# Reordering VectorE sums around the token products and the changes of batch in a routed-attention and MLP-mixer kernel

## The chip, the core and the metric

The kernel runs on one core of one Trainium2 chip. The metric is the device time of one launch in microseconds. Before the change it is 838.61 us, the median of three runs that lie between 838.55 and 838.67 us. The profiled execution took 838.92 us, of which the profile's span, from the first to the last instruction, is 837.0 us, at a granted TensorE clock of 0.999 of full speed.

## What is computed

Two blocks follow each other. The first is attention with a routing mask: 4 batches, 8 heads, 768 positions, 64 values per head; a query sees only the keys that have the same nearest centroid. The second is an MLP mixer over the 4 x 768 x 512 result. The change touches only the second:

```python
def _moe_ref(x, w_tok1, w_tok2, w_ch1, w_ch2):      # x: (4, 768, 512)
    xt = x.transpose(0, 2, 1)
    h = np.maximum(xt @ w_tok1, 0.0) @ w_tok2       # 768 -> 256 -> 768, along the tokens
    u = x + h.transpose(0, 2, 1)
    h2 = np.maximum(u @ w_ch1, 0.0) @ w_ch2         # 512 -> 1536 -> 512, along the channels
    return (u + h2).astype(np.float32)
```

All of it is float32 on the chip.

## The kernel before

The matrix products of the mixer are done by Winograd's form of Strassen's scheme: both factors are cut into 2 x 2 blocks, and seven block products replace eight. It needs sums of blocks of the left factor (S1 to S4) and of the right factor (T1 to T4) beforehand, and VectorE (DVE in the profile) makes them. T3 and S3 are written over a block that is not needed afterwards. Three of the seven products of the first channel matrix are themselves split once more in the same way; the kernel calls these the sets, with sums of their own in narrower tiles.

```python
def winograd_left(a):
    yield lambda: add(a["S1"], a["A21"], a["A22"])
    yield lambda: sub(a["S2"], a["S1"], a["A11"])
    yield lambda: sub(a["S3"], a["A11"], a["A21"])
    yield lambda: sub(a["S4"], a["A12"], a["S2"])

def winograd_right(b):
    yield lambda: sub(b["T1"], b["B12"], b["B11"])
    yield lambda: sub(b["T2"], b["B22"], b["T1"])
    yield lambda: sub(b["T3"], b["B22"], b["B12"])
    yield lambda: sub(b["T4"], b["B21"], b["T2"])
```

`left_sums(part)` makes S1 to S4 of one third of w_ch1 (four instructions of 128 x 512), `u_sums()` makes T1 to T4 of u transposed (four of 128 x 768), `set_right_sums()` the sums of u for the sets (four of 128 x 384, then four of 128 x 192), and `token_sums` those of the hidden layer of the tokens (four of 128 x 512). `winograd_left` and `winograd_right` are lists of steps, so that a step can be placed among other work: `between()` takes one step from the list `others` after each product.

The seven products accumulate in PSUM banks and are taken out step by step: a product whose bank already holds an earlier one may start only after VectorE has added that earlier state to its destination.

```python
def by_turns(n, product, of, done=None, last=False, after=()):
    # order: p1 0, p1 1, p1 2, p5 0, p5 1, p5 2, c11 0, c11 1, u2 0, u2 1, u2 2, c12 0, c12 1,
    #        c22 0, c22 1, c22 2, c12 2, c11 2, c21 0, c21 1, c21 2
    for m in range(len(order) // 2):
        ...
        if name in FIRST:                       # p1, p5, c11 begin a bank
            banks[tag, i] = ptile(tag, n)
        product(banks[tag, i], a, r, i, name in FIRST)
        x = of(to, i)
        add(x, banks[tag, i], x)                # VectorE, from PSUM
        ...
        if m in after:
            after[m]()
        between()
```

The token products run for two batches at a time, first b = 0 and 1, then 2 and 3. Beside those of 2 and 3 ScalarE (ACT) copies u of batch 0 for its transposition by DMA (`turning`), and the last pieces of w_ch2 are rounded to float32 (`weights`):

```python
for b in (0, 2):
    tok1(b, 0)                                  # 12 matmuls, then a relu on ACT
    ...
    tok1(b, 1)
    take(weights, 2)
    if b == 2:
        take(turning, 4)                        # copies of u, on ACT
    tok1(b + 1, 0)                              # the third relu
    token_sums(b, 0)                            # T1
    take(weights, len(weights) if b == 2 else 1)
    if b == 2:
        left_weights()
        take(list(left_sums(0)), 4)             # S1 to S4 of w_ch1, first third
        nc.sync.dma_start(spill, xs[1])         # x of batch 1 to DRAM, 1.5 MB
    tok1(b + 1, 1)                              # the fourth relu
    token_sums(b, 1)                            # T2, T3, T4
    if b == 2:
        take(turning, len(turning))
        usums = u_sums()
        tok2_chunks(b, {13: lambda: (next(usums), next(usums))})
    else:
        tok2_chunks(b)
        turning = list(u_steps(0))
```

After that the four batches go through the channel matrices, in the order 0, 2, 3, 1, each in three parts of w_ch1 and w_ch2. `ch1_pair` makes the first product of a part and `ch2_chunks` the second:

```python
for n, b in enumerate(batches):
    for part in range(3):
        ...
        if first:
            others += [lambda: next(usums)] * 2
            for steps in (right_weights(0), left_sums(1), set_left_sums(1)):
                others += steps
        ch1_pair(part, not first, ...)
        ...
        if part == 2 and not last:
            after[3] = lambda: take(turning, len(turning))
            after[15] = lambda: next(usums)     # T1 of the next batch's u
            usums = u_sums()
        ch2_chunks(b, part, last, after)
        between(len(others))
        if part == 2 and not last:              # the change of batch
            for _ in range(3):
                next(usums)                     # T2, T3, T4
            for step in set_right_sums():       # eight steps
                step()
```

The head of `ch1_pair` at a change of batch, in the order of its products:

```python
big(X[0], "A11", "B11", 0); big(X[1], "A11", "B11", 1)   # each big() calls between()
big(Z[0], "S1", "T1", 0)
set_(yc[:, n0], "Y", "c11"); set_(yc[:, n1], "Y", "c12")
add(a11[:, 0], yc, a11[:, 0])
set_x("Y", "Y", "p1", a11[:, 0, n0])            # product, then the add from its bank
big(Z[1], "S1", "T1", 1)
set_x("Y", None, "u2", a11[:, 0, n1])           # same bank: waits for the add above
set_z("Y", ptile("Y", HS // 2), a11)
big(X[0], "S2", "T2", 0)
...
set_x("Y", None, "c22", ...); ...               # needs T3 of the sets
big(X[1], "S2", "T2", 1)
set_x("Y", None, "c21", ...); ...               # needs T4 of the sets
```

Of the kernel before, what the change touches and what calls it, by code (L numbers as in the profile page):

```python
# [50 lines left out]
def kernel(  # L51
# [29 lines left out]
    nc = tc.nc  # L81
# [51 lines left out]
    spill = spilled.tile([P, NJ, DM], F32, name="spill")  # L133
    xs = [(x1pool if b == 1 else xpool).tile([P, NJ, DM], F32, name=f"x{b}") for b in range(B)]
# [415 lines left out]
    def sub(dst, a, b):  # L550
        nc.vector.tensor_tensor(out=dst, in0=a, in1=b, op=ALU.subtract)
# [4 lines left out]
    def left_weights():  # L556

        w = W["ch1"]
        half = DCH // 2
        A = pools["A"] = {  # L560
            f"A{i + 1}{j + 1}": w[:, 2 * j : 2 * j + 2, half * i : half * i + half]
            for i in range(2)
            for j in range(2)
        }
        extra = pools["wsums"].tile([P, 3, 2, half], F32, name="w1s")
        A["S1"], A["S2"], A["S4"] = (extra[:, i] for i in range(3))
        A["S3"] = A["A21"]
# [13 lines that stand above are left out]
    def left_sums(part):  # L581

        cols = slice(part * P, part * P + P)
        return winograd_left(
            {k: x.rearrange("p f (r c) -> p f r c", r=2)[:, :, :, cols] for k, x in pools["A"].items()}
        )
# [3 lines left out]
    def set_lefts():  # L590
        if "l2" not in pools:
            pools["l2"] = pools["w2sums"].tile([P, 3, 3, HS], F32, name="w1ss")
        A, l2 = pools["A"], pools["l2"]
        both = W["ch1"].rearrange("p f (i r c) -> p f i r c", i=2, r=2)[:, 2:4]
        single = A["S4"].rearrange("p f (r c) -> p f r c", r=2)
        for blocks, sums_ in (
            ([both[:, f, :, r] for r in range(2) for f in range(2)], [l2[:, 0:2, m] for m in range(3)]),
            ([single[:, f, r] for r in range(2) for f in range(2)], [l2[:, 2, m] for m in range(3)]),
        ):
            yield dict(  # L600
                zip(("A11", "A12", "A21", "A22", "S1", "S2", "S4", "S3"), blocks + sums_ + blocks[2:3])
            )

    def set_left_sums(part):
        cols = slice(part * P, part * P + P)
        for blocks in set_lefts():
            yield from winograd_left({k: x[..., cols] for k, x in blocks.items()})
# [13 lines left out]
    def set_right_sums():  # L621
        pools["r2"] = pools["w2sums"].tile([P, 3, 3, HS // 2], F32, name="uTss")
        for blocks in set_rights():
            yield from winograd_right(blocks)
# [33 lines left out]
    def right_weights(part):  # L658


        w = W["ch2"]
        if part == 0:
            extra = pools["w2sums"].tile([P, 3, NCT // 2, DM // 2], F32, name="w2s")
            B_ = pools["B"] = {
                f"B{i + 1}{j + 1}": w[:, 6 * i : 6 * i + 6, 256 * j : 256 * j + 256]
                for i in range(2)
                for j in range(2)
            }
            B_["T1"], B_["T2"], B_["T4"] = (extra[:, i] for i in range(3))
            B_["T3"] = B_["B12"]  # L670
        b = {name: x[:, part : NCT // 2 : NCT // 4] for name, x in pools["B"].items()}
        yield lambda: sub(b["T1"], b["B12"], b["B11"])
        yield lambda: sub(b["T2"], b["B22"], b["T1"])
        yield lambda: sub(b["T3"], b["B12"], b["B22"])
        yield lambda: sub(b["T4"], b["B21"], b["T2"])
# [23 lines left out]
    def u_steps(b):  # L699


        order = (0, 1, 4, 5, 6, 7, 2, 3)
        for i in order[:UCOLS]:
            yield lambda i=i: u_take(b, i)
        for m, i in enumerate(order):
            yield lambda i=i: u_put(i)
            if m + UCOLS < len(order):
                yield lambda m=m: u_take(b, order[m + UCOLS])
# [15 lines left out]
    late, others = [], []  # L724
# [32 lines left out]
    def tok2_chunks(b, after=()):  # L757

        A, R = pools["AT"], pools["RT"]

        def product(psum, a, r, i, start):
            nc.tensor.matmul(  # L762
                psum, lhsT=A[a][:, i], rhs=R[r], start=start, stop=True,
                skip_group_check=not start,
            )

        def of(to, i):
            return xs[b + int(to[2]) - 1][:, HJ * (int(to[1]) - 1) + i]

        by_turns(DM, product, of, after=after)  # L770
# [321 lines left out]
    def take(steps, n):  # L1092
        for _ in range(n):
            steps.pop(0)()


    for b in (0, 2):
        tok1(b, 0)
        if b == 0:
            take(weights, 1)  # L1100
            pair_put(NPAIR - 1)
            pair_out(NPAIR - 1)
            assert not state
            attention.close()
            pools["wsums"] = pool("wsums", 1, side="right")
            pools["u"] = pool("upool", 1, side="right")
            token_stack = fast.enter_context(ExitStack())
            pools["tsums"] = pool("tsums", 1, token_stack, side="right")
            take(list(token_weights()), 4)
        else:  # L1110
            take(turning, UCOLS)
            take(weights, 2)
        tok1(b, 1)
        take(weights, 2)
        if b == 2:
            take(turning, 4)
        tok1(b + 1, 0)
        token_sums(b, 0)
        take(weights, len(weights) if b == 2 else 1)
        if b == 2:  # L1120
            left_weights()
            take(list(left_sums(0)), 4)
            nc.sync.dma_start(spill, xs[1])
        tok1(b + 1, 1)
        token_sums(b, 1)
        if b == 2:
            take(turning, len(turning))
            usums = u_sums()
            tok2_chunks(b, {13: lambda: (next(usums), next(usums))})
        else:  # L1130
            tok2_chunks(b)
            turning = list(u_steps(0))
    assert not weights
    token_stack.close()
# [5 lines left out]
    for n, b in enumerate(batches):  # L1140
        turning = []
        for part in range(3):
            first, last = n == 0 and part == 0, n == B - 1 and part == 2
            if part == 2 and not last:
                turning = list(u_steps(batches[n + 1]))
            if first:
                others += [lambda: next(usums)] * 2
                for steps in (right_weights(0), left_sums(1), set_left_sums(1)):
                    others += steps
            ch1_pair(part, not first, [turning.pop(0) for _ in turning[:UCOLS]])  # L1150
            if first:
                others += list(set_right_sums()) + list(right_weights(1))
            if n == 0 and part == 1:
                for steps in (left_sums(2), set_left_sums(2), right_weights(2)):
                    others += steps
            if n == 0 and part == 2:
                others += set_left_sums(0)
            if last:
                both = fits_load()
            after = {}  # L1160
            if part == 2 and not last:
                after[3] = lambda: take(turning, len(turning))
                after[15] = lambda: next(usums)
# [3 lines that stand above are left out]
            if n == 0 and part < 2:  # L1167
                (fits_count if part else fits)()
            if part == 2 and not last:
                for _ in range(3):  # L1170
                    next(usums)
                for step in set_right_sums():
                    step()
                if n == 0:
                    xs[1] = xpool.tile([P, NJ, DM], F32, name="x0")
                    nc.sync.dma_start(xs[1], spill)
# [212 lines left out]
```

## Time and profile before

| what | value |
|---|---|
| time, median of 3 | 838.61 us |
| span of the profile | 837.0 us |
| TensorE (PE) matmuls busy | 820.4 us, 98% |
| VectorE busy | 606.3 us, 72% |
| ScalarE busy | 381.3 us, 46% |
| 315 to 356 us, token products of batches 0 and 1 | PE busy 41.00 of 41.00 us |
| 356 to 398 us, token products of batches 2 and 3 | PE busy 39.28 of 42.00 us |
| 398 to 472 us, channel products, first batch, parts 0 and 1 | PE busy 72.42 of 74.00 us |
| 472 to 837 us, the rest | PE busy 354.88 of 365.00 us |

In the lines of the timeline shown below, a line begins with the start and the length in us, then come the engine, the line of the kernel, the operation, the tile written and those read, partitions x elements, and the count of instructions merged into the line; brackets at the end give the idle time of the engine before it and who ended it. In the list of waits, a line gives the engine that waited, its line, the engine and line that ended the wait, the total in us, how often, and the longest. A matmul's listed end is modelled, so the distance from one start to the next is the better measure of its cost: it is 0.43 us for a 128 x 512 matmul of the token products, for instance (six start in 2.58 us).

### The profile page before, as it was taken

The page shows a single profiled execution, that of the slowest core. Times are in us where ns is not written, and L with a number is a line of the kernel's source. Part 1 is how long each engine was busy: PE and PEld are TensorE (multiplying, and loading weights), DVE is VectorE, ACT ScalarE, POOL GpSimd, SP SyncE. Part 2 cuts the span into 40 slices and gives each one's busy share as a digit, 9 for nine tenths or more (in the row PEclk, how much of TensorE's full clock was granted, in tenths as well). Part 3 has the DMA queues.
Part 4 walks back from the last instruction along what each step waited for, and adds up shares of the span by engine and source line. Part 5 has one row for each costly group of instructions (what it writes and reads, how often), then busy time and mean ns, then how long its engine had stood idle before and what let it go on. Part 6 is the DMA issues. An engine that isn't in the chain of part 4 may idle for free.

```text
span 837.0 us, 11463 instructions
## 1 busy us (share of the span) xinstructions
PE 820.4 (98%) x4285; PEld 526.1 (63%) x4285; DVE 606.3 (72%) x1124; ACT 381.3 (46%) x562; POOL 30.7 (4%) x28
## 2 busy tenths in 40 slices
PE   9999999999999999998999999999999999999996
PEld 5444444444444444443578787878878788787875
DVE  6879898989898878749786676655667456664654
ACT  5678677787877774054202253121541204511120
POOL 1001010101101000000000000000000000000000
PEclk9999999999999999999999999999999999999999
DMA  9887566868675335034000125000230001400002
GB/s 152 150 149 152 119 139 129 166 131 161 145 141 127 83 95 150 20 79 123 0 1 1 19 39 170 1 0 10 38 105 1 1 1 28 123 1 0 1 2 79
DMA packets 184256, 63.39 MB, mean 76 GB/s; under 512 B 172800, under 2 KB 176896, under 8 KB 183936
## 3 DMA queue, kind: packets, MB, share of 16 engines
q1 hardware_dynamic: 182592, 62.18, 34.4%
q8 instruction: 35, 0.57, 0.3%
q10 hardware_dynamic: 1600, 0.39, 0.2%
q14 instruction: 29, 0.24, 0.1%
HBM read 36.21 MB, written 7.86 MB: 53 GB/s over the span
## 4 chain that ended last, share of the span: by engine, by line
PE 86%; DVE 7%; ACT 2%; DMA 2%; issue 1%; SPq 0%; ACTq 0%; DVEq 0%
PE sc L419 19%; PE av L444 14%; PE pX L940 13%; PE pX L788 11%; PE pZ L940 6%; PE pY L801 4%; PE pY L940 3%; PE ph L523 3%; PE pZ L788 3%; PE pZ L801 3%; DVE x L554 2%; PE pX L801 2%; DMA ucols<-urows 1%; PE small L480 1%; PE pX L762 1%
## 5 line engine op out<-in xcount | busy, mean ns | idle before, releaser
L426 ACT ACTIVATE ex<-sc 128x768 f32<-128x768 f32 x192 | 151.0, 812 | 28.9 <-PE sc L419 16.9
L419 PE MATMUL sc<-qkT 64*128 64x384 f32 x768 | 155.0, 482 | 0.0
L434 DVE TENSOR_TENSOR sum<-sum,ex 128x768 f32<-128x768 f32 x128 | 127.8, 998 | 26.9 <-ACT ex L426 14.3
L444 PE MATMUL av<-ex,va 128*64 128x384 f32 x768 | 127.4, 488 | 0.0
L554 DVE TENSOR_TENSOR x<-pX,x 128x256 f32<-128x256 f32 (+1 forms) x168 | 76.2, 459 | 41.2 <-PE pX L940 39.7
L444 PEld LDWEIGHTS av<-ex,va 128*64 128x64 f32 x768 | 53.7, 137 | 71.8 <-issue 65.9
L419 PEld LDWEIGHTS sc<-qkT 64*128 64x128 f32 x768 | 67.9, 187 | 38.4 <-issue 38.3
L828 ACT COPY hA<-pX 128x384 f32<-128x384 f32 x24 | 11.5, 479 | 147.8 <-PE pX L788 143.0
L554 DVE TENSOR_TENSOR hA<-pY,hA 128x192 f32<-128x192 f32 (+1 forms) x90 | 36.7, 408 | 54.1 <-PE pY L801 39.6
L810 ACT ACTIVATE hA<-hA 128x768 f32<-128x768 f32 x35 | 29.5, 844 | 87.1 <-DVE hA L554 87.1
L788 PE MATMUL pX<-uT,wc 128*128 128x384 f32 x192 | 68.0, 487 | 0.5 <-DVE x L554 0.5
L419 PE MATMUL sc<-ohT 64*128 64x384 bf16 x384 | 62.7, 323 | 0.1
L788 PEld LDWEIGHTS pX<-uT,wc 128*128 128x128 f32 x192 | 35.7, 190 | 18.3 <-issue 1.3
L451 ACT COPY avrows<-av 128x768 uint16<-128x768 uint16 x32 | 25.5, 797 | 45.0 <-PE av L444 45.0
L554 DVE TENSOR_TENSOR x<-pZ,x 128x256 f32<-128x256 f32 (+1 forms) x84 | 36.4, 456 | 13.0 <-PE pZ L940 12.5
L523 PE MATMUL ph<-x,wt 128*128 128x512 f32 x96 | 41.6, 593 | 0.0
L419 PEld LDWEIGHTS <-ohT 64*128 64x128 bf16 x384 | 18.6, 94 | 34.2 <-issue 9.4
L940 PE MATMUL pX<-wc,hA 128*128 128x256 f32 x144 | 37.2, 381 | 1.6 <-ACT hA L925 1.2
L697 ACT COPY uT<-ucols 128x768 uint16<-128x768 uint16 x32 | 33.1, 1050 | 4.6 <-DMA ucols<-urows 4.6
L940 PE MATMUL pY<-wc,hA 128*128 128x256 f32 x144 | 35.1, 379 | 0.0
L940 PE MATMUL pZ<-wc,hS 128*128 128x256 f32 x144 | 35.0, 379 | 0.0
L788 PE MATMUL pX<-uTs,w1s 128*128 128x384 f32 x96 | 34.9, 486 | 0.0
(178 smaller groups left out, 1267.8 us busy)
## 6 DMA issues: line engine op xcount, KB each, us to landing
raw<-in_moe_w_ch_dram SPq DMA_DIRECT2D x24, 512.0 KB, 4.4
va<-in_v_dram SPq DMA_DIRECT2D x16, 384.0 KB, 3.7
out_dram<-x SPq DMA_DIRECT2D x24, 256.0 KB, 2.5
qk<-in_k_dram SPq DMA_DIRECT2D x60, 96.0 KB, 3.9
qk<-in_q_dram SPq DMA_DIRECT2D x60, 96.0 KB, 3.5
raw<-in_moe_w_tok_dram SPq DMA_DIRECT2D x3, 512.0 KB, 4.3
raw<-in_moe_w_tok_dram SPq DMA_DIRECT2D x4, 384.0 KB, 3.8
spill<-x SPq DMA_DIRECT2D x1, 1536.0 KB, 5.9
```

Source lines behind the costliest of these rows:

```text
L419: nc.tensor.matmul(sc[:, h, 0:HS], lhsT=src[rows, 1, j], rhs=src[rows, 0, js], start=start, stop=not start,)
L426: nc.scalar.activation(out=ex, in_=sc[:, :, 0:HS], func=ACT.Exp, scale=SM_SCALE)
L434: nc.vector.tensor_tensor(out=acc, in0=acc if j > 1 else st["ex", qh, 0], in1=st["ex", qh, j], op=ALU.add)
L444: nc.tensor.matmul(av[h * D : (h + 1) * D], lhsT=st["va"][:, h, j], rhs=ex[:, h], start=(j == 0), stop=(j == NJ - 1),)
L451: nc.scalar.copy(out=st["rows"][:, qh], in_=av.bitcast(U16).rearrange("p (t w) -> p w t", w=2))
L523: nc.tensor.matmul(pf, lhsT=W["tok1"][:, j, t * P : (t + 1) * P], rhs=xs[b][:, j], start=(j == 0), stop=(j == NJ - 1),)
L554: nc.vector.tensor_tensor(out=dst, in0=a, in1=b, op=ALU.add)
L697: nc.scalar.copy(out=out, in_=pools.pop(("ucols", i)).rearrange("p w j t -> p w (j t)"))
L788: nc.tensor.matmul(psum, lhsT=A[a][:, k, c], rhs=R[r][:, k], start=start and k == 0, stop=k == 1, skip_group_check=not start,)
L801: nc.tensor.matmul(psum, lhsT=left[which][a][:, part * P : part * P + P], rhs=right[which][r], start=start, stop=True, skip_group_check=no ...
L810: nc.scalar.activation(out=x, in_=x, func=ACT.Relu)
L940: nc.tensor.matmul(psum, lhsT=h2[a][:, k, i * P : (i + 1) * P], rhs=Bw[w][:, part + 3 * k], start=start and k == 0, stop=k == 1, skip_grou ...
```

## The change

The change computes the same values; it moves work in the instruction order of VectorE, ScalarE and the DMA queue. Its parts are:

1. The first third of the sums of w_ch1, `left_sums(0)`, is made among the adds of the token products of batches 0 and 1, and no longer between the sums of the hidden layer of batches 2 and 3.
2. The second third, `left_sums(1)`, is made ahead of the third relu's sum T1, and no longer in part 0 of the first batch.
3. Of the four steps of `turning` ahead of the third relu none is left there; two go behind it, the others behind the fourth.
4. x of batch 1 is written to DRAM as soon as it is complete, ahead of the transpositions of u, and no longer among them.
5. At a change of batch the sums are put into the order in which products use them: T1 and T2 of the sets first, then T2 of u at once; T3 and T4 of u and the other six steps of the sets go among the products of the next batch.

```diff
         tok1(b, 1)
         take(weights, 2)
         if b == 2:
-            take(turning, 4)
+            take(list(left_sums(1)), 4)
         tok1(b + 1, 0)
         token_sums(b, 0)
         take(weights, len(weights) if b == 2 else 1)
         if b == 2:
-            left_weights()
-            take(list(left_sums(0)), 4)
-            nc.sync.dma_start(spill, xs[1])
+            take(turning, 2)
         tok1(b + 1, 1)
         token_sums(b, 1)
         ...
         else:
+            left_weights()
+            others += left_sums(0)
             tok2_chunks(b)
+            nc.sync.dma_start(spill, xs[1])
             turning = list(u_steps(0))
 ...
             if first:
                 others += [lambda: next(usums)] * 2
-                for steps in (right_weights(0), left_sums(1), set_left_sums(1)):
+                for steps in (right_weights(0), set_left_sums(1)):
                     others += steps
 ...
             if part == 2 and not last:
-                for _ in range(3):
-                    next(usums)
-                for step in set_right_sums():
-                    step()
+                steps = list(set_right_sums())
+                for m in range(2):
+                    steps[m]()
+                next(usums)
+                others += [lambda: next(usums)] * 2
+                others += [lambda m=m: (steps[m](), steps[m + 1]()) for m in (2, 4, 6)]
```

## The prediction, written before the changed kernel was run

> **What bounds the kernel now.** I read the busy times first, then the list of TensorE's waits from 310 us on, then the timeline of TensorE and VectorE around each of those waits.
>
> ```profile
> PE 820.4 (98%) x4285; PEld 526.1 (63%) x4285; DVE 606.3 (72%) x1124; ACT 381.3 (46%) x562; POOL 30.7 (4%) x28
> ```
>
> TensorE is the bound, with matmuls in flight for 98% of the span. The change removes no matmul, so it can only return time in which TensorE stands still. These are all its waits in the mixer:
>
> ```profile
> PE pY L801 <- DVE hA L554: 3.3, 3, 1.1
> PE pX L762 <- DVE x L554: 2.2, 2, 2.0
> PE pX L940 <- ACT hA L925: 1.2, 2, 0.6
> PE pX L788 <- DVE x L554: 0.5, 1, 0.5
> PE pX L940 <- ACT hA L886: 0.4, 1, 0.4
> PE pX L762 <- ACT h L527: 0.2, 1, 0.2
> ```
>
> The first is the change of batch: three times, one per change. The second, fourth and sixth lie in the token products of batches 2 and 3 and right behind them. The two on L940 wait for ScalarE and are no aim of the change. Since ends of matmuls are modelled, these waits come out short, and I measure from start to start instead. First the token products:
>
> ```profile
> 376.02 1.88 PE L762 MATMUL pX<-h,wt 128*128 128x512 f32 x4
> ...
> 381.60 1.88 PE L762 MATMUL pY<-h,wt 128*128 128x512 f32 x4
> 385.49 2.84 PE L762 MATMUL pX<-h1s,wt2s 128*128 128x512 f32 x6 [2.01 <-DVE x L554]
> ```
>
> ```profile
> 377.55 0.69 DVE L551 TENSOR_TENSOR h1s<-h,h 128x512 f32<-128x512 f32 x1 [3.14 <-ACT h L527]
> 378.16 0.42 DVE L214 TENSOR_SCALAR wh<-wh 128x512 f32<-128x512 f32 x1
> ...
> 380.41 0.68 DVE L554 TENSOR_TENSOR w1s<-wc 128x512 f32<-128x512 f32 x1
> ...
> 384.75 1.88 DVE L554 TENSOR_TENSOR x<-pX,x 128x512 f32<-128x512 f32 x3
> ```
>
> Four matmuls from 381.60 at 0.43 us end at 383.32; the next started at 385.49, 2.17 us late. It accumulates into the bank of the first product, whose add VectorE began only at 384.75. VectorE stood idle until 377.55 and from then on is packed (7.81 us busy from 377.5 to 385.5): T1, a rounding of weights, four sums of w_ch1, T2 to T4, the adds. The whole stage has 21 products of two matmuls, 42 x 0.43 = 18.06 us, and would end at 394.08 from its start at 376.02; the first channel matmul started at 398.27, so 4.19 us are lost in all. Now one change of batch:
>
> ```profile
> 512.54 1.45 PE L788 MATMUL pZ<-uTs,w1s 128*128 128x384 f32 x4
> 515.10 0.92 PE L801 MATMUL pY<-uTss,w1ss 128*128 128x192 f32 x4 [1.11 <-DVE hA L554]
> ```
>
> ```profile
> 508.24 0.95 DVE L551 TENSOR_TENSOR uTs<-uT,uTs 128x768 f32<-128x768 f32 x1
> ...
> 510.84 0.55 DVE L551 TENSOR_TENSOR uTss<-uT 128x384 f32<-128x384 f32 x1
> ...
> 514.03 0.55 DVE L554 TENSOR_TENSOR hA<-pX,hA 128x384 f32<-128x384 f32 x1
> 514.69 0.36 DVE L554 TENSOR_TENSOR hA<-pY,hA 128x192 f32<-128x192 f32 x1
> ```
>
> Four 128x384 matmuls take 1.29 us (the group before began at 510.28 and its successor at 511.57), so u2 could start at 513.83; it started at 515.10, 1.27 us late. The add it waits for stands behind eleven sums, 508.24 to 514.03. The other two changes show the same lateness (622.50 and 729.88, each behind a group that began 2.56 us earlier).
>
> **What the Trainium skill says.** "TensorE: Matmul & The Clock Gate", section "Architectural detail: the array is 16× 32×32, not 1× 128×128", says that ScalarE and VectorE are strict FIFO. The trace agrees: products of 377 us were added at 384.75, and the third relu ran at 376.93 though its matmuls were over near 371. Hence mere position in the stream is worth time. "Perfetto Trace Analysis", section "DVE / Act Engine Instruction (TENSOR_ADD, Activation, etc)", says a VectorE record runs from the start in the ALUs to the write's acknowledgement. That fits 0.69 us per record while packed 128x512 sums start 0.60 us apart; I count the distances. "VectorE: DVE Perf Modes", section "Mode 2×_2P — use both read ports for one tensor", has float32 tensor_tensor stuck at one element per cycle; with its 0.96 GHz, 768 elements would be 0.80 us, an estimate. The trace has 0.87 us from start to start. So the sums get no cheaper by moving.
>
> **The change, part by part.**
>
> *Sums of w_ch1, first third.* Four sums, 380.41 to 382.94, leave the packed stretch: 2.53 us less ahead of the adds. They land among the adds of batches 0 and 1, one after each of the first four. VectorE's adds there start at 340.04, 0.60 us apart. With four more sums the adds of p1 0, p1 1, p1 2 start at 340.04, 341.24, 342.44, of u2 0 at about 347.24. TensorE wants the bank of p1 0 at 344.26 (add done 340.7) and that of u2 0 at 348.55 (done 347.9). The smallest margin I find is that 0.6 us, so this costs nothing; VectorE has 18.0 us for 25 x 0.60 = 15.0 us.
>
> *Sums of w_ch1, second third.* Four more, ahead of T1. VectorE was idle from the end of a rounding, last start 373.72 plus 0.61, so from 374.33, to 377.55. They take 2.53 us: 374.33 to 376.86. They fit, if T1's input is there by then.
>
> *The relu ahead of the copies.* The third relu now follows ScalarE's rounding steps directly, at about 373.66 instead of 376.93, and is done at 374.2. T1 therefore starts at 376.86 instead of 377.55, 0.69 us earlier. One pair of copies (0.91 + 0.73 us) stands between third and fourth relu and ends at 375.85, before the fourth relu's matmuls are done (376.18); so that relu runs at 376.4 and the 0.32 us that TensorE lost at 378.06 goes too.
>
> *Sum for this stage.* T1 at 376.86, rounding from 377.47 for 2.25 us, T2 to T4 from 379.72 for 1.81 us, first add at 381.53 instead of 384.75: 3.22 us earlier. Its bank is free at 382.2, and u2 0 is due at 382.90: the long wait goes. But from there to the end VectorE, and no longer TensorE, sets the pace: before, adds and two sums of u ran packed from 384.75 to the add of c21 0 at 397.44, and the first channel matmul came 0.83 us later, at 398.27. The same 12.69 us from 381.53 give 394.22 and the matmul at 395.05. **Gain 3.22 us of the 4.19**, the rest stays as waits in the last products. The copies of u, finished at 390.7 before, will finish near 387, ahead of the two sums of u (389.9).
>
> *The spill.* It leaves the middle of the transpositions (378.31, where ScalarE then waited 2.94 us for one) for about 353, when the queue is empty until 362.17. TensorE did not wait for it, so no gain by itself; it makes the copies safe at their new, later place.
>
> *Part 0 of the first batch.* Four sums fewer; TensorE waits there only on ScalarE (L940). Gain 0.
>
> *Change of batch.* VectorE from 508.24, by the distances of the trace: T1 and T2 of the sets 0.59 + 0.47, then T2, T3, T4 of u 3 x 0.87, then T3 and T4 of the sets 2 x 0.47, gives 512.85 for the a11 add instead of 514.03: the four narrow steps, 1.19 us, now come behind it. Its product is done by then (its matmuls start at 511.57 and 511.89). So u2 starts at 515.10 - 1.18 = 513.92, still 0.09 us late. The postponed steps cost 0.6 us twice, where VectorE idled 0.69, 0.89 and 1.91 us. Three changes: **3.54 us**.
>
> Total 3.22 + 3.54 = 6.76 us; 838.61 - 6.76 = 831.9 us.
>
> **Rivals.** (a) A transposition takes the place of the removed wait. The first step at a change of batch now reads the last copied columns of u. ScalarE's last copy ended at 508.23 in the first change, 0.01 us before VectorE wants it, but at 614.4 against 615.63 in the second and 722.3 against 723.02 in the third. One change may lose some 0.1 us; a late DMA more. I would see 832 to 832.5. (b) ScalarE becomes the chain: if the copies of u behind the fourth relu were late, the sums of u at 389.9 would wait and up to 3 us of the stage would return, 834 to 835. Against it: 3 us of reserve, and no spill beside them. (c) The four sums put into batches 0 and 1 delay accumulation there. That needs margins below my 0.6 us; 0 to 1 us. (d) The waits are hidden anyway, because a late TensorE meets a later wait. Against it: after each, TensorE runs without a gap for many us, so each is on the path that sets the end.
>
> **Range and chances.** The two halves are arithmetic on distances that repeat to 0.01 us in the three changes. My doubt is mostly of waits not foreseen, which lengthen: 830.8 to 834.0 us. Two per cent would be 16.8 us, more than twice the 7.8 us of all waits listed above; so "within 2%" is nearly certain.
>
> **What would show it.** In the new timeline: first add of the token products of 2 and 3 near 381.5; first channel matmul near 395.05; no wait of 2 us on L762; short waits left on the last L762 products or L788; three waits on L801 of 0.1 us or none; TensorE's waits on L940 unchanged. I am wrong if batches 0 and 1 show new TensorE waits, if T1 starts after 377, or if VectorE waits for ScalarE ahead of the sums of u.

## The result and the profile after

The changed kernel takes 832.46 us, the median of six runs from 831.93 to 832.70 us; the kernel before, 838.57 us in six runs from 838.25 to 838.67. The ratio is 0.9927, with a 95% interval of 0.9914 to 0.9940: about 6.1 us, where 6.76 were predicted (831.9 us, range 830.8 to 834.0).

TensorE's list of waits from 310 us on, which had six lines:

```profile
PE pX L940 <- ACT hA L925: 1.2, 2, 0.6
PE pX L788 <- DVE x L554: 0.5, 1, 0.5
PE pX L940 <- ACT hA L886: 0.4, 1, 0.4
PE pX L940 <- DVE x L554: 0.2, 1, 0.2
```

The 3.3 us on L801 and the 2.2 us on L762 are gone from it; the waits for ScalarE stand as they were. The last line is no new delay: that matmul, at 461.23, starts 2.04 us after the group of eight before it (459.19), and its counterpart before, at 465.03, also started 2.04 us after its group of eight (462.99). The start of the token products of batches 2 and 3, in TensorE's timeline, and their end:

```profile
375.56 2.74 PE L762 MATMUL pX<-h,wt 128*128 128x512 f32 x6
...
380.71 1.88 PE L762 MATMUL pY<-h,wt 128*128 128x512 f32 x4
382.42 2.74 PE L762 MATMUL pX<-h1s,wt2s 128*128 128x512 f32 x6
...
394.45 2.82 PE L788 MATMUL pX<-uT,wc 128*128 128x384 f32 x8 [0.50 <-DVE x L554]
```

From 380.71 to 382.42 are 1.71 us, four matmuls at their pace: the second product on the first bank starts without delay. The stage, from its first matmul to the first channel matmul, takes 394.45 - 375.56 = 18.89 us, against 398.27 - 376.02 = 22.25 us before. VectorE in the same stretch:

```profile
373.74 0.68 DVE L554 TENSOR_TENSOR w1s<-wc 128x512 f32<-128x512 f32 x1
...
376.27 0.69 DVE L551 TENSOR_TENSOR h1s<-h,h 128x512 f32<-128x512 f32 x1
...
380.93 1.88 DVE L554 TENSOR_TENSOR x<-pX,x 128x512 f32<-128x512 f32 x3
```

The second third of the sums of w_ch1 now runs ahead of T1, T1 follows without idling, and the first add comes 5.37 us after the stage's first matmul instead of 8.73. Now the first change of batch, TensorE and then VectorE:

```profile
508.75 1.45 PE L788 MATMUL pZ<-uTs,w1s 128*128 128x384 f32 x4
510.31 0.92 PE L801 MATMUL pY<-uTss,w1ss 128*128 128x192 f32 x4
```

```profile
504.44 0.55 DVE L551 TENSOR_TENSOR uTss<-uT 128x384 f32<-128x384 f32 x1
505.10 0.56 DVE L551 TENSOR_TENSOR uTss<-uT,uTss 128x384 f32<-128x384 f32 x1
...
507.31 0.95 DVE L551 TENSOR_TENSOR uTs<-uT,uTs 128x768 f32<-128x768 f32 x1
508.29 0.56 DVE L551 TENSOR_TENSOR uT<-uT 128x384 f32<-128x384 f32 x1
...
509.24 0.55 DVE L554 TENSOR_TENSOR hA<-pX,hA 128x384 f32<-128x384 f32 x1
```

From 508.75 to 510.31 are 1.56 us for a group of 1.29 us, so u2 is 0.27 us late, not 1.27. The list of waits does not show it: the listed end of that group (508.75 + 1.45 = 510.20) covers all but 0.11 us of it, so only the distance between starts does. At the second and third change the distance is 1.56 and 1.57 us.

Three changes at 1.0 us and 3.36 us in the token products make 6.36 us. The medians differ by 6.1 us. Scatter of this size lies ahead of the mixer, in code that the change does not touch: the first matmul of the mixer stood anywhere from 316.2 to 316.8 us in the profiles of this study. That it makes up the remaining 0.3 us is not shown, since only one execution of each kernel was profiled.

### The profile page after: what moved, and what is told of

The parts are those of the page before. It is cut to its first block, busy times and chain, and to the rows that moved or that the text cites. A ratio compares the mean times of both kernels' runs of the same rounds, so it can differ in the third digit from the quotient of the medians.

```text
span 830.0 us, 11458 instructions
## 1 busy us (share of the span) xinstructions
PE 818.9 (99%) x4285; PEld 525.7 (63%) x4285; DVE 606.2 (73%) x1124; ACT 381.3 (46%) x562; POOL 30.7 (4%) x28
## 4 chain that ended last, share of the span: by engine, by line
PE 90%; DVE 7%; issue 1%; ACT 0%; DMA 0%; SPq 0%; DVEq 0%; ACTq 0%
PE sc L419 18%; PE pX L940 14%; PE av L444 13%; PE pX L788 11%; PE pZ L940 7%; PE ph L523 5%; PE pY L801 4%; PE pY L940 4%; PE pZ L788 3%; PE pZ L801 3%; PE pX L762 2%; PE pX L801 2%; PE small L480 1%; DVE x L554 1%; DVE sum L434 1%; PE pZ L762 1%
## 5 line engine op out<-in xcount | busy, mean ns | idle before, releaser
L788 PE MATMUL pX<-uT,wc 128*128 128x384 f32 x192 | 68.0, 487 | 0.5 <-DVE x L554 0.5
L788 PEld LDWEIGHTS pX<-uT,wc 128*128 128x128 f32 x192 | 35.7, 190 | 18.3 <-issue 1.3
L940 PE MATMUL pX<-wc,hA 128*128 128x256 f32 x144 | 37.2, 381 | 1.6 <-ACT hA L925 1.2
L940 PE MATMUL pY<-wc,hA 128*128 128x256 f32 x144 | 35.1, 379 | 0.0
L940 PE MATMUL pZ<-wc,hS 128*128 128x256 f32 x144 | 35.0, 379 | 0.0
L788 PE MATMUL pX<-uTs,w1s 128*128 128x384 f32 x96 | 34.9, 486 | 0.0
```

Of the source, the lines that this page charges most:

```text
L788: nc.tensor.matmul(psum, lhsT=A[a][:, k, c], rhs=R[r][:, k], start=start and k == 0, stop=k == 1, skip_group_check=not start,)
L940: nc.tensor.matmul(psum, lhsT=h2[a][:, k, i * P : (i + 1) * P], rhs=Bw[w][:, part + 3 * k], start=start and k == 0, stop=k == 1, skip_grou ...
```

## The experiments

In each comparison, the "stage" is the time from the first token product of batches 2 and 3 to the first channel matmul, taken from TensorE's timeline as above; where the attention part ends does not enter it. It has a scatter of its own: four profiles whose order in the stage is that of the changed kernel gave 18.73 to 19.01 us, so that differences of 0.2 us in it say nothing by themselves. All kernels below compute the whole result. Times are medians of 4 to 8 runs.

**The two halves, each alone.** The first kernel is the one before with the new order at the changes of batch; the second is the changed kernel with that order undone.

```diff
 # new order at the changes of batch, alone
-                for _ in range(3):
-                    next(usums)
-                for step in set_right_sums():
-                    step()
+                steps = list(set_right_sums())
+                for m in range(2):
+                    steps[m]()
+                next(usums)
+                others += [lambda: next(usums)] * 2
+                others += [lambda m=m: (steps[m](), steps[m + 1]()) for m in (2, 4, 6)]
```

> The kernel before with the new order at the changes of batch alone. Theory (the add that the second-level product u2 waits for comes out of VectorE's stream 1.0 us earlier at each of three changes, and the two halves of the change do not touch each other): 3.0 us faster than before, 835.6 us, with u2 0.27 us late at each change as in the changed kernel, and the token products as before (first channel matmul 22.25 us after the first token product of batches 2 and 3). Rival (the parts help each other, so one alone brings less, or the wait moves to a later product of the same part): under 2 us, with new waits on L801 or L788 behind u2.

Measured: 836.08 us against 838.71 for the kernel before on the same chip, ratio 0.9970 (0.9959 to 0.9981). The stage took 22.08 us, and u2 was 0.27 us late at each change.

> The changed kernel with the old order at the changes of batch: only the token products' stage is changed. Theory: 3.36 us faster than before (the stage takes 18.89 us instead of 22.25), 835.2 us, and the three waits of 1.27 us at the changes of batch are back. Rival (the time that TensorE saves here is given back at the first change of batch or in part 0): under 2.5 us in the total although the stage itself takes 18.9 us.

Measured: 835.78 us, ratio 0.9967 (0.9955 to 0.9979). The stage took 19.01 us, and u2 was again 1.28 us late at each change. The two gains, 2.6 and 2.9 us, sum to 5.6, a little under the changed kernel's 6.1, and within the scatter of the medians; the distances in the timelines are those of the changed kernel. The halves do not touch each other, and nothing is given back later: from the first channel matmul to the end of the span it takes 438.8 us here and 438.7 in the kernel before, and 435.8 us with the new order at the changes of batch alone against 435.6 in the changed kernel.

**Which part of the token products' half matters.** First the sums alone, with relus, copies and spill of the kernel before:

```diff
         if b == 2:
+            take(list(left_sums(1)), 4)
             take(turning, 4)
 ...
-            left_weights()
-            take(list(left_sums(0)), 4)
             nc.sync.dma_start(spill, xs[1])
 ...
         else:
+            left_weights()
+            others += left_sums(0)
             tok2_chunks(b)
 ...
-                for steps in (right_weights(0), left_sums(1), set_left_sums(1)):
+                for steps in (right_weights(0), set_left_sums(1)):
```

> The kernel before with the eight sums of w_ch1 moved (first third to batches 0 and 1, second third ahead of T1), but relus, copies of u and spill where they were. Theory (the stage's loss is the length of VectorE's packed stream from T1 on): T1 still at its old distance, because its relu still stands behind the copies; the stream is four sums shorter, so adds and first channel matmul come 2.53 us earlier: 836.0 us. Rival (what counts is ScalarE, whose relu stood behind the copies of u): no gain worth naming, 838.3 us or more.

Measured: 836.27 us, ratio 0.9971 (0.9960 to 0.9983). The stage took 395.76 - 375.96 = 19.80 us, 2.45 us less than before. VectorE's timeline of this kernel:

```profile
376.19 0.69 DVE L551 TENSOR_TENSOR w1s<-wc,w1s 128x512 f32<-128x512 f32 x1
377.57 0.69 DVE L551 TENSOR_TENSOR h1s<-h,h 128x512 f32<-128x512 f32 x1 [0.69 <-ACT h L527]
```

Four sums less in the packed stretch, and T1 where it was, waiting 0.69 us for its relu: as the theory says. Then the relu alone:

```diff
         if b == 2:
-            take(turning, 4)
 ...
             take(list(left_sums(0)), 4)
             nc.sync.dma_start(spill, xs[1])
+            take(turning, 2)
         tok1(b + 1, 1)
```

> The kernel before with the copies of u behind the third relu alone; sums and spill as before. Theory: T1's relu is done at the distance of the changed kernel and VectorE is free there, so T1 starts 3.2 us earlier than before (at about 374.33 instead of 377.55), the packed stream behind it is as long as before, and adds and first channel matmul come 3.2 us earlier: 835.4 us, as much as the whole of the stage's change, so that the moved sums add almost nothing to it. Rival (sums are what counts, as the prediction had it: 2.53 us for them and 0.69 us for the relu): 0.7 us, 837.9 us. Second rival (the spill beside the copies then delays the sums of u): gain under 2 us with a wait of VectorE on ScalarE ahead of them.

Measured: 836.31 us, ratio 0.9974 (0.9963 to 0.9984), a stage of 395.74 - 375.75 = 19.99 us. That is 2.26 us less than before: far more than the 0.7 us of the rival, but about 1 us less than the theory. Why is in the timelines of ScalarE and VectorE:

```profile
373.26 0.68 ACT L207 ACTIVATE wh<-raw 128x512 f32<-128x512 f32 x1 [0.79 <-DMA raw<-in_moe_w_ch_dram]
...
374.41 0.57 ACT L527 ACTIVATE h<-ph 128x512 f32<-128x512 f32 x1
```

```profile
375.02 0.69 DVE L551 TENSOR_TENSOR h1s<-h,h 128x512 f32<-128x512 f32 x1 [0.63 <-ACT h L527]
```

The third relu (L527) stands behind the rounding of the last piece of w_ch2, that piece now came late from DRAM, and T1 waits for the relu. My second rival had the spill right but its victim wrong: it did not delay the copies of u. So the spill was tried by itself.

**The spill.** The changed kernel with the spill in its old place of the program:

```diff
         if b == 2:
+            nc.sync.dma_start(spill, xs[1])
             take(turning, 2)
 ...
             tok2_chunks(b)                       # batches 0 and 1
-            nc.sync.dma_start(spill, xs[1])
```

> The changed kernel with the write of x of batch 1 back in its old place, among the transpositions of u. Theory (TensorE does not wait for it; the copies of u have 1.5 to 3 us to spare): the last copies of u come up to 4 us later, VectorE's sums of u at the same time, total 832.5 us within 0.3. Rival (the spill was what held things up): the sums of u wait for ScalarE and the stage takes 1 to 3 us more, 833.5 to 835.5 us.

Measured: 832.62 us, ratio 0.9927 (0.9914 to 0.9941), so no difference in the total that could be told from the changed kernel's 832.46; but the profiled run had a stage of 395.79 - 376.06 = 19.73 us, 0.84 longer. The total was as the theory expected, the stage as neither did, and one profile could be an exception. So it was run again beside the changed kernel itself, and beside a third kernel in which the spill stands one line lower, behind `take(turning, 2)`:

> The changed kernel once more, beside the three others of this group on the same chip. Both theories: stage of the token products 18.9 to 19.0 us, 832.4 us.

> The changed kernel with the write of x of batch 1 in its old place, once more, beside the changed kernel itself. Theory: pieces of w_ch2 land in 5.3 us, third relu 0.8 us later, stage 19.7 us, total 0.8 us above the changed kernel of the same group. Rival (the first profile was an exception): total equal within 0.3 us and a stage of 18.9 us.

> The changed kernel with the write of x of batch 1 behind the first of the late copies of u, so that the queue issues it only after a transposition that waits for ScalarE (about 375 us), when the two last pieces of w_ch2 have landed. Theory (what cost 0.8 us of the stage with the write in its old place of the program was that it shared the DMA engines with those two pieces, since nothing held it back in the queue any more): pieces land in 4.2 us again, stage 18.9 to 19.0 us, total as the changed kernel within 0.3. Rival (the write costs because it stands ahead of transpositions of u): stage 19.7 us or more, 833.2 us.

Measured: the changed kernel 832.33 us with a stage of 18.73; the spill in its old place 832.73 with 395.37 - 376.13 = 19.24; the spill one line lower 832.39 with 18.87 (ratios to before 0.9928, 0.9931 and 0.9927). The old place costs 0.4 us of the median (831.46 to 832.52 us against 832.47 to 832.76), half of what was expected, and 0.5 us of the stage. The confidence intervals of the ratios overlap, so the totals alone would not show it; but both profiles with the old place, 19.73 and 19.24 us, lie above all others of this order. The DMA issues between 366 and 380 us, with size and time to landing, of the kernel with the spill in its old place:

```profile
spill<-x SPq DMA_DIRECT2D x1, 1536.0 KB, 8.9
raw<-in_moe_w_ch_dram SPq DMA_DIRECT2D x2, 512.0 KB, 5.0
```

and of the kernel with the spill one line lower:

```profile
spill<-x SPq DMA_DIRECT2D x1, 1536.0 KB, 5.9
raw<-in_moe_w_ch_dram SPq DMA_DIRECT2D x2, 512.0 KB, 4.2
```

In the kernel before, the spill stood in the queue behind transpositions that waited for ScalarE's copies, so it was issued at 378.31, when the last pieces of w_ch2 had landed. With the copies moved behind the relu nothing holds it any more: the queue issues it at 368.32, directly behind the two loads.

```profile
367.27 1.00 SPq L201 DMA_DIRECT2D raw<-in_moe_w_ch_dram  x2
368.32 0.42 SPq L1121 DMA_DIRECT2D spill<-x  x1
```

The write and the two loads are then in flight together, the pieces take 0.8 us longer to land, and their rounding comes later. Here the delay does not pass through the third relu, since T1 follows the moved sums without idle time: VectorE's rounding, which stands ahead of these sums and waits for ScalarE, begins 3.83 us ahead of the stage instead of 4.33 in the changed kernel beside it, and these 0.50 us are what the stage takes longer. The kernel with the spill one line lower settles it: there the spill is again among the transpositions (issued at 376.90), and costs nothing. Then the relu's move together with the early spill, without any moved sums:

```diff
         if b == 2:
-            take(turning, 4)
 ...
             take(list(left_sums(0)), 4)
-            nc.sync.dma_start(spill, xs[1])
+            take(turning, 2)
 ...
             tok2_chunks(b)
+            nc.sync.dma_start(spill, xs[1])
             turning = list(u_steps(0))
```

> The kernel before with the copies of u behind the third relu and the write of x of batch 1 directly behind the token products of batches 0 and 1; the sums of w_ch1 stay as before. Theory (the relu's place is worth 3.2 us by itself, and in the run with the relu alone 1.0 us of it was lost to the write beside the last pieces of w_ch2): stage 18.9 to 19.1 us, 3.2 us faster than before, 835.4 us. Rival (without the moved sums the stage cannot come below 19.8): 836.2 us.

Measured: 834.95 us against 838.36 on the same chip, ratio 0.9959 (0.9945 to 0.9972), a stage of 395.12 - 376.04 = 19.08 us. With both in place the relu alone is worth 3.17 of the 3.36 us, and the 0.19 us between them are no gain of the moved sums. It shows when the count begins at VectorE's last rounding ahead of T1, which starts 4.05, 4.18 and 3.98 us ahead of the stage in the kernel before, the changed kernel and this one:

```profile
371.97 0.43 DVE L214 TENSOR_SCALAR wh<-wh 128x512 f32<-128x512 f32 x1 [0.73 <-ACT wh L207]
371.38 0.43 DVE L214 TENSOR_SCALAR wh<-wh 128x512 f32<-128x512 f32 x1 [0.60 <-ACT wh L207]
372.06 0.43 DVE L214 TENSOR_SCALAR wh<-wh 128x512 f32<-128x512 f32 x1 [0.79 <-ACT wh L207]
```

From there to the first channel matmul it takes 26.30, 23.07 and 23.06 us. Once the relu and the spill have moved, the moved sums of the changed kernel bring nothing: four sums stand in the packed stretch either way, ahead of T1 or behind it.

**Are the moved sums worth anything, then?** If T1's relu is early, the four sums of the second third stand in its way. They go back to part 0:

```diff
         if b == 2:
-            take(list(left_sums(1)), 4)
 ...
-                for steps in (right_weights(0), set_left_sums(1)):
+                for steps in (right_weights(0), left_sums(1), set_left_sums(1)):
```

> The changed kernel with the second third of the sums of w_ch1 back in part 0 of the first batch. Theory (these four sums now stand ahead of T1 in VectorE's stream while T1's relu is already done, and in part 0 they are free): T1 starts 2.53 us earlier than in the changed kernel, TensorE and no longer VectorE sets the pace to the end of the token products, the stage takes 18.06 us instead of 18.89, the wait on L788 is gone, total 831.6 us. Rival (the move of the second third is needed, because part 0 is then short of VectorE time): the stage is shorter but new waits of TensorE on VectorE appear in part 0 or 1, total 832.4 us or more.

Measured: 831.11 us, ratio 0.9914 (0.9900 to 0.9927), a stage of 393.93 - 375.90 = 18.03 us. VectorE and TensorE in this kernel:

```profile
374.41 0.68 DVE L551 TENSOR_TENSOR h1s<-h,h 128x512 f32<-128x512 f32 x1
...
388.12 0.69 DVE L554 TENSOR_TENSOR x<-pX,x 128x512 f32<-128x512 f32 x1 [0.17 <-PE pX L762]
```

```profile
393.93 2.77 PE L788 MATMUL pX<-uT,wc 128*128 128x384 f32 x8
```

T1 starts at 374.41, right behind the rounding; the adds catch up with TensorE and from then on wait for it; the channel matmul starts without a wait. In part 0 TensorE's list of waits had no new line. The second third's move costs 0.86 us (0.70 to 0.98 against the four profiles with the changed kernel's order). This rests on the timelines: the interval of the ratio overlaps that of the changed kernel, and the 1.35 us between the medians are more than the stage accounts for. The first third's move stays useful: up to the end of this stage this kernel differs from the one with relu and spill alone only in the sums of the first third, and its stage is 18.03 us against 19.08.

**The rest of the wait at a change of batch.** T3 and T4 of the sets go one product later, so that they stand behind the add that u2 waits for:

```diff
-                others += [lambda: next(usums)] * 2
+                others += [lambda: next(usums)] * 2 + [lambda: None]
```

> The changed kernel with T3 and T4 of the sets one product later at a change of batch, so that they stand behind the add that u2 waits for. Theory (what is left of the wait, 0.27 us and 0.10 us of restart at each change, is those two steps, of 0.47 us each, plus their wait for T4 of u): u2 starts without a wait, three times 0.3 to 0.37 us, total 831.4 us. Rival (u2 waits for the product ahead of the add, not for VectorE): the add does not come earlier and the wait stays, 832.4 us. Second rival: the later steps make the product c22 wait instead.

Measured: 831.69 us, ratio 0.9914 (0.9900 to 0.9927). VectorE and TensorE at the first change:

```profile
507.87 0.95 DVE L551 TENSOR_TENSOR uTs<-uT,uTs 128x768 f32<-128x768 f32 x1
509.25 0.56 DVE L554 TENSOR_TENSOR hA<-pX,hA 128x384 f32<-128x384 f32 x1 [0.43 <-PE pX L801]
```

```profile
509.31 1.45 PE L788 MATMUL pZ<-uTs,w1s 128*128 128x384 f32 x4
510.60 0.81 PE L801 MATMUL pY<-uTss,w1ss 128*128 128x192 f32 x4
```

VectorE now waits for the product, and u2 starts 1.29 us behind the group before it, without a delay, at the other two changes too. No wait appeared behind it. Here as well the timelines carry the finding, since the intervals of the ratios overlap. At last both improvements together:

> The changed kernel with both: second third of the sums of w_ch1 back in part 0, and T3 and T4 of the sets one product later. Theory: the two gains add, 0.83 + 1.0 us, total 830.6 us; TensorE then waits in the mixer only for ScalarE (L940). Rival: they do not add, 831.4 us or more.

Measured: 830.72 us, ratio 0.9906 (0.9891 to 0.9921), a stage of 18.03 us and no wait at the changes of batch. It is the fastest version of this study, about 1.7 us below the changed kernel (832.46 and 832.33 in the two other groups); its slowest run, 830.82, is faster than the changed kernel's fastest, 831.46. TensorE's list of waits in its mixer has only the three lines on L940 that the changed kernel has, with the same figures.

## Why the prediction was right, point by point

*Token products of 2 and 3.* Predicted 3.22 us, measured 3.36. The chain was as told: the first add 5.37 us behind the stage's start, predicted 5.51, and the long wait gone; the end of the stage set by VectorE, with 0.50 us of wait on L788. The 0.14 us of difference come from ahead of the moved sums: the rounding before them began 4.18 us ahead of the stage's start, not 4.05 as in the kernel before. Counted from that rounding, the end of the stage came 26.30 - 23.07 = 3.23 us earlier, which is the forecast.

*Sums and relu.* The step that split this gain into 2.53 us for the sums and 0.69 us for the relu was wrong, although its total was right, since the changed kernel has both in place. T1 starts when both its relu is done and VectorE has come to it, so the parts are under a maximum, not in a sum: sums alone gave 2.45 us, the relu with the early spill 3.17, all three 3.36, and the last two are alike when counted from the rounding. "They fit", said of the second third, took VectorE's idle time from the kernel before, where it lasted to 377.55; with the relu early it is no longer idle time, and the sums there cost 0.86 us.

*The spill.* "No gain by itself" was not tried: no run moves the spill alone in the kernel before. But with the copies moved it was needed: in its old place it cost about 0.4 us of the median, and 0.9 us of the stage where T1 follows its relu directly (19.99 against 19.08 us without the moved sums). That a transfer is held back by what it stands behind in the queue, and is let loose when that moves, was missed.

*Sums among the products of batches 0 and 1.* Predicted free; those products ran from 336.93 to 354.96 us in the changed kernel, 18.03 us, TensorE's pace. Rival (c) falls.

*Part 0.* Predicted free; the waits on L940 are the same, apart from the line that was shown above to be no new delay.

*Change of batch.* Predicted 0.09 us late, measured 0.27, three times: 3.0 us in place of 3.54. The mis-sized term is the sum of distances ahead of the a11 add: 509.24 - 504.44 = 4.80 us, not 4.61. T1 to T2 of the sets took 0.66 instead of 0.59, and T4 of u to T3 of the sets 0.98 instead of 0.87. Both pairs now stand beside other instructions than those from which I took the distances. Why that makes 0.07 and 0.11 us is not shown. A late copy on ScalarE is not the reason for the first: at the second change the last copy ended at 609.56, well before T1 of the sets at 610.84, and T2 still came 0.65 us after T1. That the two steps T3 and T4 of the sets were what kept u2 waiting is shown by the run that moves them.

*Rivals.* (a) did not come: VectorE began the sums at 504.44, directly behind its last add. (b) did not come in the changed kernel: the sums of u started packed at 389.30. But the copies of u ended at 387.81, so the reserve was 1.5 us and not 3. (d) falls: the gains of stage and changes add up to the whole.

## What to carry to other kernels

Where an engine works strictly in order, ask of every step which consumer waits behind it, and put first what the bounding engine needs first. When two moves both advance one start, their gains are under a maximum: try each alone before keeping both, since one may be in the other's way, as four sums here were. And when instructions move, look at what stood behind them in a DMA queue: what was held back may now start beside a load that matters.

## What was not expected of the hardware

A 1.5 MB write to DRAM issued beside two 512 KB loads took 8.9 us to land instead of 5.9, and the loads 5.0 instead of 4.2. Two pairs of float32 sums on VectorE came 0.07 and 0.11 us further apart in the new order than in the old, at each of the three changes of batch, which made 0.54 us.
